# A gated mix of attention and a gMLP: whole-array products, shared key moments and a new order of loads

## The chip, the cores and the metric

The kernel runs on one core of one Trainium2 chip. The metric is the device time of one execution in microseconds (us). The core has five engines that run side by side, each through its own list of instructions in a fixed order: TensorE (PE in the profile; its weight loads are shown apart as PEld), VectorE (DVE), ScalarE (ACT), GpSimd (POOL) and SyncE (SP), which issues the DMAs. They wait for each other by semaphores.

## What is computed

`x` is 2048 x 512. A gate `g` weighs two branches. Branch a is attention with 32 heads of 16 dimensions that share one key and one value head. Branch b is a gMLP: a gelu, a layer norm over half of the columns, a product over the sequence with `w_sp`, and a gated projection.

```python
x = A_x
g = _sigmoid((x * gate_w).sum(-1, keepdims=True))
a = _A_ref(x, A_wq, A_wk, A_wv, A_wo)     # q @ k, softmax, @ v, then @ wo; 32 query heads, one k and v
b = _B_ref(x, B_w_in, B_w_sp, B_b_sp, B_w_out)
# inside _B_ref:
#   z = gelu(x @ w_in); z1 = z[:, :688]; z2 = layernorm(z[:, 688:])
#   out = (z1 * (w_sp @ z2 + b_sp)) @ w_out
return g * a + (1 - g) * b
```

The scores are small, so the kernel replaces the exponential by a polynomial of third degree. Numerator and denominator of the softmax then need only moments of the keys (sums over the 2048 positions of products of key components, with and without the value), computed once, and per query the products of its components.

## The kernel before

**Planner and queues.** The program is a list of tasks, each with an engine, an estimated cost, what it reads and writes, and a priority (a lower `pri` goes first). `Plan.run` (L241) plays them through a model of the engines and so fixes, when the program is built, the order of each engine's list. On the chip each engine keeps that order: an instruction that waits holds up what stands behind it. `after` makes a real wait, `opens` and `gates` only hold a task back in the model. SP's list of DMAs comes out of the same planning.

**Products.** `mm4` (L477 to 482) writes a product as four matmuls of 128 rows by 32 columns of the array, each with its own weight load, on the same moving data; they run side by side and are called a quad here. `mm1` (L485) uses the whole array of 128 by 128 in one matmul. `mmq` (L487 to 492) is a quad whose four parts have different weights or different moving data, and `half5` (L759 to 764) one whose parts take two halves of the moving data. In the profile L480 is `mm4`, L485 `mm1`, L490 `mmq`, L762 `half5`.

**Start.** Loads are issued in the order identity, first quarter of x, wk, wv, gate_w, second quarter, wq, the other quarters, win2 (the half of w_in for z2), constants, win1 (the half for z1) (L523 to 535). Per quarter, `g_x` transposes x, `g_kv` makes keys and values (and, with a 33rd column, the gate's sums), `moments` (L593 to 602) adds to the key moments, and `g_gate` makes the gate's sums in another layout. `moments` has per tile of 128 positions the large product for the third moments (bank K3), a correction, and three small quads that make the lower moments four times over for four groups of partitions (bank T). `moments_out` turns them into the weights T3, T3d, M2, T1b, T2b, TEb. `gate_out` runs the exponentials (L634 to 636), and the gelus of z2 (L746) come after them by `after=[ex_t[0]]`.

**Units.** There are 16 units u, each one group of eight heads by one quarter of the queries. `g_q` (L641) makes Q and writes it to DRAM (`qe`, four DMAs and a fifth for a rolled copy); `y_load` (L659) reads it back twice for each half e of a unit, spread over partitions, as Y and YB. POOL multiplies them to X (L691), two products with T3 follow (W, L696), and DVE multiplies their results by Y to Pr (L698). N and D, in banks of their own, then collect Q times T1b and T2b, E times TEb, X times M2 and T3d, and Pr times `sel` (L701 to 711); M2, T3d and `sel` are `mmq` quads. After each four units `g_den` (L717) makes the denominators and writes OT (L735).

**gMLP.** `g_z2` (L739) makes z2 with gelu, statistics, a power on POOL for the inverse deviation (L752, priority 0) and the normalisation on ACT (L756). `g_z1` makes z1. `g_sp` (L787) multiplies by the transposed `w_sp`, which comes in quarters by transposing DMAs (`ld_wT`, L776) into the space of x and of the key features. `g_out` (L817) makes four output tiles of each quarter.

**Order at the end of the builder (L835 to 883).** The four quarters of the start, moments and gate; then Q of units 0 to 3, all of z2, all of z1; then the units, with Q four units ahead, `w_sp` after units 0 and 1, the late weights (`ld_late`) after unit 2, and per four units `g_den`, `g_sp`, `g_out`.

Of the kernel before, what the change touches and what calls it, by code (L numbers as in the profile page):

```python
# [34 lines left out]
WARM = 5  # L35
# [7 lines left out]
SLACKS = {("pool", "pe"): 1200.0, ("dve", "pe"): 350.0, ("act", "pe"): 300.0}  # L43
# [3 lines left out]
DMA_ISSUE = 300.0  # L47


def constants():  # L50
# [29 lines left out]
    rol = np.eye(128) + bmq * ((p[:, None] + 8) % 16 == p[None, :] % 16)  # L80
# [4 lines left out]
    small = np.concatenate([sel.reshape(128, 128), hsel.reshape(128, 128), bmq, rol], 1)  # L85
# [103 lines left out]
class Task:  # L189
    __slots__ = ("alt", "fn", "deps", "users", "left", "pri", "grp", "first", "dma", "bytes", "chan", "tag", "idx",  # L190
                 "ready", "eng", "start", "end", "op", "rate", "opens", "gates")


class Plan:
# [8 lines left out]
    def add(self, eng, cost, fn, r=(), w=(), pri=50.0, grp=None, evac=False, dma=0, size=0, chan=None, rate=DMA_RATE, tag="", after=(), opens=()):  # L203
# [5 lines left out]
        t.users, t.op, t.eng = [], None, None  # L209
        r, w = list(r), list(w)  # L210
# [16 lines left out]
        t.gates = []  # L227
        for d in t.deps:
            d.users.append(t)
        for d in t.opens:  # L230
            d.users.append(t)
        t.left = len(t.deps) + len(t.opens)
# [8 lines left out]
    def run(self, prog, allowed):  # L241
# [5 lines left out]
        pipe = [0.0]  # L247
        busy = {e: 0.0 for e in ENG}
# [42 lines left out]
        while done < len(self.tasks):  # L291
# [51 lines left out]
            if t.dma:  # L343
                free[e] = now + cost
                st = max(pipe[0], now + DMA_ISSUE)
                pipe[0] = st + t.bytes / t.rate
# [24 lines left out]
def build_kernel(nc, x_d, wq_d, wk_d, wv_d, wo_d, win_d, wsp_d, bsp_d, wout_d, gw_d, out_d):  # L371
    es = ExitStack()
    with es:
# [32 lines left out]
        cs = sb("cs", [128, 512], B16)  # L406
# [10 lines left out]
        T1d = sb("T1d", [128, 1], F32)  # L417
        S0 = sb("S0", [128, 1], F32)
# [45 lines left out]
        rol = cs[:, 384:512]  # L464
        x2 = x_d.rearrange("b s d -> (b s) d")
        out2 = out_d.rearrange("b s d -> (b s) d")

        def diag(t):

            a = t[:, :, :]  # L470
            return bass.AP(tensor=a.tensor, offset=a.offset, ap=[a.ap[0], [48, 2], [1, 16]])
# [4 lines left out]

        def mm4(b, n, off, lhsT, rhs, start, stop):  # L477

            def f(t):
                return [t.matmul(ps[32 * q:32 * q + 32, 512 * b() + off:512 * b() + off + n], lhsT[:, 32 * q:32 * q + 32], rhs,  # L480
                                 start=start, stop=stop, tile_position=(0, 32 * q)) for q in range(4)]
            return f
# [4 lines left out]
        def mmq(b, n, off, lhsTs, rhss, start, stop):  # L487

            def f(t):
                return [t.matmul(ps[32 * q:32 * q + 32, 512 * b() + off:512 * b() + off + n], lhsTs[q], rhss[q],  # L490
                                 start=start, stop=stop, tile_position=(0, 32 * q)) for q in range(4)]
            return f
# [8 lines left out]
        nd = [0]  # L501

        def load(eng, fn, w, r=(), size=0, n=1, pri=0.0, chan=None, rate=DMA_RATE, tag="", after=()):
# [3 lines left out]
            return add(eng, 4500.0 if rate < DMA_RATE else 540.0 * n, fn, r=r, w=w, dma=16 * n, size=size, pri=pri, chan=chan, rate=rate, tag=tag, after=after)  # L507
# [8 lines left out]
        add("dve", 350.0, lambda v: v.memset(Pr[:, 0, 0, :], 0.0), w=[("Pr", 0)], pri=-1)  # L516
        gw_ = Group("any")
# [5 lines left out]
        load("sp", lambda q: q.dma_start(ident[:], id_d), ["id"], size=32768, pri=-1)  # L523
# [3 lines left out]
        load("sp", nonc(lambda q: q.dma_start(wkvg[:, :, 32:33], gw_d.rearrange("(dt p one) -> p dt one", p=128, one=1))), ["gw"], size=16384, pri=0)  # L527
        ld_x(1)
        load("sp", lambda q: q.dma_start(wq[:], wq_d.rearrange("(dt p) n -> p dt n", p=128)), ["wq"], size=524288, pri=1)
        ld_x(2)  # L530
        ld_x(3)
        load("sp", lambda q: q.dma_start(win[:, :, FH:F], win_d[:, FH:F].rearrange("(dt p) n -> p dt n", p=128)), ["win2"], size=704512, pri=4)
        load("sp", lambda q: q.dma_start(cf[:], cf_d), ["cf"], size=8704, pri=5)
        load("sp", lambda q: q.dma_start(cs[:], cs_d), ["cs"], size=131072, pri=5)
        load("sp", lambda q: q.dma_start(win[:, :, 0:FH], win_d[:, 0:FH].rearrange("(dt p) n -> p dt n", p=128)), ["win1"], size=704512, pri=6)
        add("pool", 300.0, lambda g: g.memset(bspz[:], 0.0), w=[("bspz", 0), ("bspz", 1)], pri=0)
        add("pool", 100.0, lambda g: g.memset(nhalf[:], -0.5), w=["nhalf"], pri=0)
        add("pool", 100.0, lambda g: g.memset(RK[:, :, 304:305], 1.0), w=["rk1"], pri=0)
        add("pool", 1600.0, lambda g: g.memset(kkD, 0.0), w=[("X", c) for c in range(4)], pri=0)
# [8 lines left out]
        add("dve", 100.0, lambda v: v.tensor_copy(gwr[:], wkvg[:, :, 32:33].broadcast_to([128, 4, 32])), r=["gw"], w=["gwr"], pri=0)  # L548
# [12 lines left out]
        def g_kv(c):  # L561
            g = Group("any")
            for k in range(4):
                for dt in range(4):
                    add("pe", 26.0, mm1(lambda g=g: g.b, 33, 64 * k, xT[:, dt, 512 * c + 128 * k:512 * c + 128 * k + 128], wkvg[:, dt, 0:33], dt == 0, dt == 3),
                        r=["wk", "wv", "gw", ("x", c, dt)], grp=g, pri=0, tag="kv")
# [5 lines left out]
            add("dve", 200.0, lambda v: v.tensor_copy(RK[:, t4, 272:304].rearrange("p k (e d) -> p k e d", e=2),  # L572
                                                      src()[:, :, 16:32].unsqueeze(2).broadcast_to([128, 4, 2, 16])),
                w=[("rv", c)], grp=g, evac=True, pri=0, tag="rv")
            add("dve", 130.0, lambda v: v.tensor_scalar(RK[:, t4, 256:272], src()[:, :, 0:16], 0.25, None, ALU.mult), w=[("rk", c)], grp=g, evac=True, pri=0, tag="rk")
            add("dve", 100.0, lambda v: v.tensor_scalar(gs[:, t4].unsqueeze(2), src()[:, :, 32:33], E_MAX, None, ALU.min), w=[("gs", c)], grp=g, evac=True, pri=0, tag="gs")
            kxa = kx[:, t4, 0:16]
            kxo = bass.AP(tensor=kxa.tensor, offset=kxa.offset, ap=[kxa.ap[0], [32, 4], [1, 16], [1, 8]])
            add("dve", 620.0, lambda v: v.tensor_tensor(psi[:, t4, :].rearrange("p k (r i) -> p k r i", i=8), kxa.unsqueeze(3).broadcast_to([128, 4, 16, 8]), kxo, ALU.mult),
                r=[("kx", c)], w=[("psi", c)], pri=1, tag="psi")  # L580
            add("dve", 1150.0, lambda v: v.tensor_tensor(RK[:, t4, 0:256].rearrange("p k (c d) -> p k c d", d=16), kxa.unsqueeze(3).broadcast_to([128, 4, 16, 16]),
                                                         RK[:, t4, 272:288].unsqueeze(2).broadcast_to([128, 4, 16, 16]), ALU.mult),
                r=[("kx", c), ("rv", c)], w=[("rkv", c)], pri=1, tag="rkv")
            add("pool", 450.0, lambda v: v.tensor_tensor(kkE[:, t4, :].rearrange("p k (e d) -> p k e d", e=2), kx[:, t4, 0:16].unsqueeze(2).broadcast_to([128, 4, 2, 16]),
                                                         kx[:, t4, 8:24].unsqueeze(2).broadcast_to([128, 4, 2, 16]), ALU.mult),
                r=[("kx", c)], w=[("kkE", c)], pri=1, tag="kkE")
            add("pool", 300.0, lambda v: v.tensor_scalar(kkD[:, t4, :].rearrange("p k (r i) -> p k r i", i=8)[:, :, :, 0], kkE[:, t4, 0:16], -1.0, None, ALU.mult),
                r=[("kkE", c)], w=[("X", c)], pri=1, tag="kkE")
# [4 lines left out]
        def moments(c):  # L593
            for k in range(4):
                kt = 4 * c + k
                st, sp_ = kt == 0, kt == 15
                rep = lambda a: [a] * 4
# [538 lines left out]
```

## Time and profile before

| | |
|---|---|
| median of 3 runs | 336.86 us (334.85 to 341.41) |
| the profiled execution | 337.39 us, of which the span from first to last instruction is 335.6 us |
| PE busy | 303.2 us, 6279 matmuls |
| DVE, POOL, ACT busy | 239.7, 165.9, 93.8 us |
| moved by DMA | 54.17 MB, 161 GB/s on average |

The profile is that of one execution. The span leaves out 1.8 us around the instructions. A busy PE is not PE at its peak: a matmul's row lasts until its last result is out, and the next one starts before that. So the pace of a stream of matmuls is read from the starts of neighbouring rows.

### The profile page before, as it was taken

The page shows a single profiled execution, that of the slowest core. Times are in us where ns is not written, and L with a number is a line of the kernel's source. Part 1 is how long each engine was busy: PE and PEld are TensorE (multiplying, and loading weights), DVE is VectorE, ACT ScalarE, POOL GpSimd, SP SyncE. Part 2 cuts the span into 40 slices and gives each one's busy share as a digit, 9 for nine tenths or more (in the row PEclk, how much of TensorE's full clock was granted, in tenths as well). Part 3 has the DMA queues.
Part 4 walks back from the last instruction along what each step waited for, and adds up shares of the span by engine and source line. Part 5 has one row for each costly group of instructions (what it writes and reads, how often), then busy time and mean ns, then how long its engine had stood idle before and what let it go on. Part 6 is the DMA issues. An engine that isn't in the chain of part 4 may idle for free.

```text
span 335.6 us, 13852 instructions
## 1 busy us (share of the span) xinstructions
PE 303.2 (90%) x6279; PEld 162.9 (49%) x6279; DVE 239.7 (71%) x335; ACT 93.8 (28%) x163; POOL 165.9 (49%) x156
## 2 busy tenths in 40 slices
PE   5976879899999997999999769988999999799993
PEld 2763345454445554564445335542565554244551
DVE  1855479998465798876949859849588977949522
ACT  2525467966655010113212002230100012000001
POOL 7421049656757284367484614376672487640000
PEclk9977899999999999999999999999999999999998
DMA  6956264999996899398999752988987579700002
GB/s 160 348 160 170 72 130 120 190 199 283 189 215 156 199 165 237 94 189 158 263 187 233 185 120 42 238 187 209 248 153 177 109 177 240 172 5 2 4 4 66
DMA packets 54472, 54.17 MB, mean 161 GB/s; under 512 B 36900, under 2 KB 45960, under 8 KB 54280
## 3 DMA queue, kind: packets, MB, share of 16 engines
q1 hardware_dynamic: 54408, 53.24, 68.6%
q8 instruction: 50, 0.82, 1.1%
q14 instruction: 14, 0.11, 0.1%
HBM read 40.65 MB, written 5.24 MB: 137 GB/s over the span
## 4 chain that ended last, share of the span: by engine, by line
PE 74%; DVE 12%; issue 6%; ACT 4%; DMA 1%; SPq 1%; DVEq 0%
PE ps L480 61%; PE ps L490 8%; DVE Pr L698 6%; PE ps L485 3%; ACT z L756 2%; PE ps L762 2%; DMA wkvg<-in_gate_w_dram 1%; ACT z L745 1%; DVE bst L747 1%; DVE z L801 1%; DVE win L735 0%; DVE nmr L753 0%; DVE Prd L713 0%; DVE Rh L728 0%; DVE outsb L828 0%
## 5 line engine op out<-in xcount | busy, mean ns | idle before, releaser
L691 POOL TENSOR_TENSOR X<-Y,YB 128x512 bf16<-128x512 bf16 x128 | 148.3, 1159 | 96.1 <-DMA Y<-qe 36.2
L698 DVE TENSOR_TENSOR Pr<-ps,Y 128x1024 bf16<-128x1024 f32 x128 | 152.3, 1215 | 32.3 <-issue 22.7
L480 PE MATMUL ps<-wT,z 128*32 128x512 bf16 x1280 | 85.0, 379 | 0.0
L480 PE MATMUL ps<-X,T 128*32 128x512 bf16 x1024 | 80.7, 380 | 4.1 <-DVE Pr L698 3.9
L480 PEld LDWEIGHTS ps<-wT,z 128*32 128x32 bf16 x1280 | 36.6, 97 | 30.0 <-issue 0.2
L480 PEld LDWEIGHTS ps<-X,T 128*32 128x32 bf16 x1024 | 26.9, 96 | 31.8 <-DVE Pr L698 12.6
L480 PE MATMUL ps<-win,xT 128*32 128x344 bf16 x512 | 25.0, 320 | 3.4 <-ACT z L745 2.9
L480 PE MATMUL ps<-wout,z 128*32 128x512 bf16 x384 | 26.2, 379 | 0.5 <-DVE z L804 0.5
L679 ACT ACTIVATE E<-ps 128x512 bf16<-128x512 f32 x16 | 9.5, 597 | 59.8 <-PE ps L480 56.1
L712 ACT ACTIVATE Ns<-ps 128x512 f32<-128x512 f32 x16 | 9.6, 599 | 58.1 <-PE ps L490 58.1
L648 ACT ACTIVATE Qt<-ps 128x512 bf16<-128x512 f32 x16 | 9.6, 597 | 47.2 <-PE ps L480 38.2
L827 ACT ACTIVATE outsb<-ps,G 128x512 bf16<-128x512 f32 x14 | 9.5, 687 | 41.5 <-PE ps L480 41.5
L480 PE MATMUL ps<-xT,win 128*32 128x512 bf16 x320 | 20.3, 380 | 0.5 <-ACT E L679 0.5
L801 DVE TENSOR_TENSOR z<-ps,z 128x512 bf16<-128x512 f32 x20 | 13.7, 683 | 9.7 <-PE ps L480 9.5
L490 PE MATMUL ps<-Pr,cs 128*32 128x512 bf16 x256 | 19.7, 379 | 0.5 <-DVE Pr L698 0.5
L735 DVE SCALAR_TENSOR_TENSOR win<-Ns,S,ps 128x512 bf16<-128x512 f32 x16 | 11.9, 745 | 10.9 <-PE ps L480 10.8
L480 PEld LDWEIGHTS ps<-win,xT 128*32 128x32 bf16 x512 | 12.6, 99 | 14.1 <-ACT z L745 7.0
L480 PE MATMUL ps<-xT,wq 128*32 128x512 bf16 x256 | 18.1, 400 | 0.6 <-ACT Q L656 0.2
L747 DVE BATCH_NORM_STATS2 bst<-z 128x6 f32<-128x344 bf16 x32 | 15.4, 505 | 4.0 <-ACT z L745 3.9
L480 PE MATMUL ps<-wo,win 128*32 128x512 bf16 x256 | 17.8, 379 | 0.0
L745 ACT ACTIVATE z<-ps 128x344 bf16<-128x344 f32 x32 | 14.0, 454 | 9.0 <-PE ps L480 7.9
L756 ACT ACTIVATE z<-z,nmr,rstd 128x688 bf16<-128x688 bf16 x16 | 15.0, 960 | 1.7 <-DVE nmr L753 1.6
(119 smaller groups left out, 314.6 us busy)
## 6 DMA issues: line engine op xcount, KB each, us to landing
Y<-qe SPq DMA_DIRECT2D x32, 512.0 KB, 5.2
YB<-qe SPq DMA_DIRECT2D x32, 512.0 KB, 6.7
wT<-in_A_x_dram SPq DMA_DIRECT2D x4, 512.0 KB, 6.1
qe<-Qt SPq DMA_DIRECT2D x64, 32.0 KB
out_dram<-outsb SPq DMA_DIRECT2D x16, 128.0 KB, 3.3
win<-in_B_w_in_dram SPq DMA_DIRECT2D x2, 688.0 KB, 8.8
qe<-qe SPq DMA_DIRECT2D x16, 64.0 KB
wout<-in_B_w_out_dram SPq DMA_DIRECT2D x1, 640.0 KB, 5.3
```

The costliest lines, as they stand in the source:

```text
L480: return [t.matmul(ps[32 * q:32 * q + 32, 512 * b() + off:512 * b() + off + n], lhsT[:, 32 * q:32 * q + 32], rhs, start=start, stop=stop, ...
L485: return lambda t: t.matmul(bank(b(), n, off), lhsT, rhs, start=start, stop=stop)
L490: return [t.matmul(ps[32 * q:32 * q + 32, 512 * b() + off:512 * b() + off + n], lhsTs[q], rhss[q], start=start, stop=stop, tile_position=( ...
L648: add({"act": (520.0, lambda a: a.activation(Qt[:, s, :], bank(g.b), ACT.Copy))}, 0, None, w=[("Q", s)], grp=g, evac=True, pri=1, tag="Qev")
L691: xf = lambda v, xi=xi, j=j, n=n: v.tensor_tensor(X[:, xi, :], Y[:, n % NY, j, :], YB[:, n % NYB, j, :], ALU.mult)
L698: add("dve", 1230.0, lambda v, gw=gw, pi=pi, n=n, j=j: v.tensor_tensor(Pr[:, pi, :, :], bank(gw.b, 1024).rearrange("p (t n) -> p t n", t=2 ...
L712: add({"act": (590.0, lambda a: a.activation(Ns[:, u % NNS, :], bank(gn.b), ACT.Copy))}, 0, None, w=[("Ns", u % NNS)], grp=gn, evac=True, ...
L735: add("dve", 750.0, lambda v, gr=gr, u=u, G=G: v.scalar_tensor_tensor(OT[:, tg % 2, G, :], Ns[:, u % NNS, :], S0[:, 0:1], bank(gr.b), ALU. ...
L745: add("act", 400.0, lambda a, g=g, h=h: a.activation(z2[:, FH * st + 344 * h:FH * st + 344 * h + 344], bank(g.b, 344), ACT.Gelu_apprx_tanh ...
L747: add("dve", 495.0, lambda v, h=h: v.bn_stats(bst[:, st, h, :], z2[:, FH * st + 344 * h:FH * st + 344 * h + 344]), r=[("z2", st, h)], w=[( ...
L756: add("act", 820.0, lambda a, s2=s2: a.activation(z2[:, FH * s2:FH * s2 + FH], z2[:, FH * s2:FH * s2 + FH], ACT.Identity, bias=nmr[:, s2:s ...
L801: add("dve", 690.0, lambda v: v.tensor_tensor(dst, bank(g.b), dst, ALU.mult), w=[("z1", ft, tc)], grp=g, evac=True, pri=3.5, tag="u")
```

## The change

1. **Whole-array products.** All `mm4` become `mm1`: Q, E, W, the products with T1b, T2b and TEb, z1, z2, `w_sp` (but for its last tile), out, and the spread of the denominators. `mmq` and `half5` stay quads. The planner adds `SWITCH` (100 ns) where PE goes from one kind to the other, and a penalty of 2.0 on the priority of a task that would switch.
2. **N and D of a quad in one run.** The products with M2 and T3d get `after=tp[3:]`, that is, they wait for the fourth Pr of their half, as those with `sel` do.
3. **Key cross-moments once, then spread.** Two whole-array products per tile in place of three quads and the correction; then `mT`, a copy in two bf16 parts, and six products with `spr` that spread them over the partitions. The key features `psi` and `rkv` may go to POOL as well as to DVE.
4. **Gate late.** gate_w is loaded after unit 0's Y loads. The gate's sums (16 quads, and 64 products of one column in `g_gs`) follow z1 in the list, and the exponentials wait for all gelus. A gelu on `ones` at the start loads its table.
5. **New order of loads.** wq follows wk; win1 comes after unit 0's loads; DMAs of units have priorities from 2.1 up, ahead of win2 (4) and of the rest. `hold` keeps others back in the model until the last Y load; no wait comes of it on the chip. The power on POOL has priority 11 in place of 0, and a `slack` of 4 us.
6. **Order of the units.** Q runs three units ahead, z1 stands after unit 0, `w_sp` quarters after units 1 and 3. Nine warming matmuls in place of five.

```diff
-WARM = 5
+WARM = 9
+SWITCH = 100.0
+YPRI = 2.1
+SWITCH_PRI = 2.0
...
-                k = (t.pri, t.idx)
+                k = (t.pri + (SWITCH_PRI if e == "pe" and t.tiles != tiles else 0.0), t.idx)
...
+            if e == "pe":
+                if t.tiles != tiles:
+                    cost += SWITCH
+                tiles = t.tiles
...
-        def mm4(b, n, off, lhsT, rhs, start, stop):
-
-            def f(t):
-                return [t.matmul(ps[32 * q:32 * q + 32, 512 * b() + off:512 * b() + off + n], lhsT[:, 32 * q:32 * q + 32], rhs,
-                                 start=start, stop=stop, tile_position=(0, 32 * q)) for q in range(4)]
-            return f
...
+        add("act", 1300.0, lambda a: a.activation(nmr[:, 0:1], ones[:, 0:1], ACT.Gelu_apprx_tanh), r=["ones"], w=["junk2"], pri=-2, tag="table")
...
+        load("sp", lambda q: q.dma_start(wq[:], wq_d.rearrange("(dt p) n -> p dt n", p=128)), ["wq"], size=524288, pri=0)
...
-                add("pe", c_mm(288), mm1(lambda: gK3.b, 288, 0, psi[:, kt, :], RK[:, kt, 0:288], st, False), r=[("psi", c), ("rkv", c), ("rk", c), ("rv", c)], grp=gK3, pri=1, tag="K3")
-                add("pe", 26.0, mm1(lambda: gK3.b, 16, 272, kkD[:, kt, :], RK[:, kt, 272:288], False, sp_), r=[("X", c), ("rv", c)], grp=gK3, pri=1, tag="K3")
-                add("pe", 30.0, mmq(lambda: gT.b, 49, 0, rep(kx[:, kt, :]), rep(RK[:, kt, 256:305]), st, False), r=[("kx", c), ("rk", c), ("rv", c), "rk1"], grp=gT, pri=1, tag="T")
-                add("pe", 26.0, mmq(lambda: gT.b, 16, 64, rep(kkE[:, kt, :]), rep(RK[:, kt, 272:288]), False, False), r=[("kkE", c), ("rv", c)], grp=gT, pri=1, tag="T")
-                add("pe", 26.0, mmq(lambda: gT.b, 1, 96, rep(RK[:, kt, 272:304]), rep(RK[:, kt, 304:305]), False, sp_), r=[("rv", c), "rk1"], grp=gT, pri=1, tag="T")
+                add("pe", c_mm(288), mm1(lambda: gK3.b, 288, 0, psi[:, kt, :], RK[:, kt, 16:304], st, sp_), r=[("psi", c), ("rkv", c), ("rk", c), ("rv", c)], grp=gK3, pri=1, tag="K3")
+                add("pe", 30.0, mm1(lambda: gT.b, 49, 0, RK[:, kt, 193:321], RK[:, kt, 272:321], st, False), r=[("rkv", c), ("rk", c), ("rv", c), "rk1"], grp=gT, pri=1, tag="T")
+                add("pe", 26.0, mm1(lambda: gT.b, 16, 49, kkD[:, kt, :], RK[:, kt, 288:304], False, sp_), r=[("X", c), ("rv", c)], grp=gT, pri=1, tag="T")
...
+            for i, (off, lo, n) in enumerate(((0, 0, 49), (64, 49, 16), (96, 48, 1))):
+                for z in range(2):
+                    add("pe", 30.0, lambda t, i=i, off=off, lo=lo, n=n, z=z: t.matmul(bank(gT2.b, n, off), spr[:, i, :], mT[:, z, lo:lo + n], start=i == 0 and z == 0, stop=i == 2 and z == 1),
+                        r=["cs", "mTh", "mTl"], grp=gT2, pri=1, tag="T2")
...
-            ex_t[0] = add("act", 2200.0, ex, r=[("gs", c) for c in range(4)], w=["Er", "E"], pri=-1, tag="gate")
+            ex_t[0] = add("act", 2200.0, ex, r=["gs"], w=["Er", "E"], pri=5, tag="gate", after=[t for t in pl.tasks if t.tag in ("gelu1", "gelu2")])
...
-                        add("pe", c_mm(512), mm4(lambda gw=gw, t=t: gw.b + t, 512, 0, T3[:, t, :], X[:, xi, :], True, True),
+                        add("pe", c_mm(512), mm1(lambda gw=gw, t=t: gw.b + t, 512, 0, T3[:, t, :], X[:, xi, :], True, True),
...
-                add("pe", c_mm(512), mmq(lambda: gn.b, 512, 0, [M2[:, e, :]] * 4, [X[:, i, :] for i in xs], False, False), r=["M2"] + xr, grp=gn, pri=pr_, tag="N")
+                add("pe", c_mm(512), mmq(lambda: gn.b, 512, 0, [M2[:, e, :]] * 4, [X[:, i, :] for i in xs], False, False), r=["M2"] + xr, grp=gn, pri=pr_, tag="N", after=tp[3:])
...
-w=[("rstd", st // 4)], pri=0, tag="pow")
+w=[("rstd", st // 4)], pri=11, tag="pow", slack=4000.0)
...
-        for u in range(4):
+        for u in range(2):
             q_and_guard(u)
         for st in range(NST):
             g_z2(st)
-        for ft in range(6):
-            for tc in range(4):
-                g_z1(ft, tc)
...
-                if u < 2:
-                    ld_wT(u)
+                if u == 0:
+                    ld_win1()
+                    for ft in range(6):
+                        for tc in range(4):
+                            g_z1(ft, tc)
...
+                    for c in range(4):
+                        g_gate(c)
+                    for st in range(NST):
+                        g_gs(st)
+                    gate_out()
+                    q_and_guard(2)
+                if u in (1, 3):
+                    ld_wT(u // 2)
                 if u == 2:
                     ld_late()
-                if u + 4 < 16:
-                    q_and_guard(u + 4)
+                if u + 3 < 16:
+                    q_and_guard(u + 3)
```

More of the change, by code (lines that the diff above doesn't have):

```diff
@@ L190 @@
     __slots__ = ("alt", "fn", "deps", "users", "left", "pri", "grp", "first", "dma", "bytes", "chan", "tag", "idx",
-                 "ready", "eng", "start", "end", "op", "rate", "opens", "gates")
+                 "ready", "eng", "start", "end", "op", "rate", "opens", "gates", "tiles", "slack")
 class Plan:
@@ L201, in __init__, with add @@
         self.readers = {}
-    def add(self, eng, cost, fn, r=(), w=(), pri=50.0, grp=None, evac=False, dma=0, size=0, chan=None, rate=DMA_RATE, tag="", after=(), opens=()):
+    def add(self, eng, cost, fn, r=(), w=(), pri=50.0, grp=None, evac=False, dma=0, size=0, chan=None, rate=DMA_RATE, tag="", after=(), opens=(), hold=(), slack=0.0):
         t = Task()
@@ L209, in add @@
         t.users, t.op, t.eng = [], None, None
+        t.tiles = getattr(fn, "tiles", 1)
         r, w = list(r), list(w)
@@ L226, in add @@
         t.opens = [self.lastw[k] for k in opens]
-        t.gates = []
+        t.gates = list(hold)
+        t.slack = slack
         for d in t.deps:
             d.users.append(t)
-        for d in t.opens:
+        for d in t.opens + t.gates:
             d.users.append(t)
-        t.left = len(t.deps) + len(t.opens)
+        t.left = len(t.deps) + len(t.opens) + len(t.gates)
         for k in r:
@@ L247, in run @@
         pipe = [0.0]
+        tiles = 1
         busy = {e: 0.0 for e in ENG}
@@ L345, in run @@
                 st = max(pipe[0], now + DMA_ISSUE)
-                pipe[0] = st + t.bytes / t.rate
+                pipe[0] = st + t.bytes / (DMA_FIRST if st < 16000.0 and t.rate == DMA_RATE else t.rate)
                 t.end = pipe[0] + DMA_LAT
@@ L491, in f @@
                                  start=start, stop=stop, tile_position=(0, 32 * q)) for q in range(4)]
+            f.tiles = 4
             return f
@@ L501, in build_kernel, with load @@
         nd = [0]
-        def load(eng, fn, w, r=(), size=0, n=1, pri=0.0, chan=None, rate=DMA_RATE, tag="", after=()):
+        yld = [None]
+        def load(eng, fn, w, r=(), size=0, n=1, pri=0.0, chan=None, rate=DMA_RATE, tag="", after=(), hold=()):
             if chan is None:
@@ L506, in load @@
                 nd[0] += 1
-            return add(eng, 4500.0 if rate < DMA_RATE else 540.0 * n, fn, r=r, w=w, dma=16 * n, size=size, pri=pri, chan=chan, rate=rate, tag=tag, after=after)
+            return add(eng, 4500.0 if rate < DMA_RATE else 540.0 * n, fn, r=r, w=w, dma=16 * n, size=size, pri=pri, chan=chan, rate=rate, tag=tag, after=after, hold=hold)
         def nonc(fn):
@@ L581, in g_kv @@
[L581 to L586, printed above, removed]
@@ L776, in ld_wT @@
         def ld_wT(tc):
-            load("sp", lambda q: q.dma_start(bspz[0:1, tc % 2, :], bsp_d[512 * tc:512 * tc + 512].rearrange("(one t) -> one t", one=1)), [("bspz", tc % 2)], size=4096, pri=13, chan="bsp%d" % (tc % 2), after=[yld[0]] if tc < 2 else [])
+            load("sp", lambda q: q.dma_start(bspz[0:1, tc % 2, :], bsp_d[512 * tc:512 * tc + 512].rearrange("(one t) -> one t", one=1)), [("bspz", tc % 2)], size=4096, pri=13, chan="bsp%d" % (tc % 2), hold=[yld[0]] if tc < 2 else [])
             for k in range(4):
@@ L790, in g_sp @@
             n = 512 if ft < 5 else 256
-            mk = mm4 if ft < 5 else half5
-            add("pe", c_mm(n), mk(lambda: g.b, 512, 0, ones, bspz[:, tc % 2, :], True, False), r=["ones", ("bspz", tc % 2)], grp=g, pri=pri, tag="sp", opens=[("z2", i, 1) for i in range(NST)] + [("wT", tc % 2, k) for k in range(4)])
+            mk = mm1 if ft < 5 else half5
+            add("pe", c_mm(n), mk(lambda: g.b, 512, 0, ones[:], bspz[:, tc % 2, :], True, False), r=["ones", ("bspz", tc % 2)], grp=g, pri=pri, tag="sp", opens=[("z2", i, 1) for i in range(NST)] + [("wT", tc % 2, k) for k in range(4)])
             for st in range(NST):
```

159 lines of the change are left out of this document (87 added, 72 removed).

## The prediction

> **What bounds the kernel now.** I read the page first (shares, slices, chain), then two long stretches, then what PE waits for, then single rows for paces.
>
> ```profile
> span 335.6 us, 13852 instructions
> ...
> PE 303.2 (90%) x6279; PEld 162.9 (49%) x6279; DVE 239.7 (71%) x335; ACT 93.8 (28%) x163; POOL 165.9 (49%) x156
> ...
> PE 74%; DVE 12%; issue 6%; ACT 4%; DMA 1%; SPq 1%; DVEq 0%
> ```
>
> PE carries three quarters of the chain and is busy for 90%; no other engine passes 71%. So the end moves by what PE is spared or what it loses. But busy is not peak, so I need the pace. The timeline of PE gives it, in a dense stretch:
>
> ```profile
> 309.59 1.68 PE L480 MATMUL ps<-wT,z 128*32 128x512 bf16 x28
> 311.10 0.39 PE L490 MATMUL ps<-Pr,cs 128*32 128x512 bf16 x4
> ...
> 50.79 0.90 PE L480 MATMUL ps<-win,xT 128*32 128x344 bf16 x20
> 51.52 0.39 PE L480 MATMUL ps<-X,T 128*32 128x512 bf16 x4
> ...
> 318.70 0.62 PE L480 MATMUL ps<-Rh,sg 128*32 128x128 bf16 x32
> 319.14 0.39 PE L480 MATMUL ps<-wo,win 128*32 128x512 bf16 x4
> ```
>
> 28 matmuls, 7 quads, lie between two starts 1.51 us apart: 0.216 us for a quad of 512 columns (0.42 ns per column). 5 quads of 344 columns take 0.73 us, 0.146 each; 8 of 128 columns 0.44 us, 0.055 each. All three are the same rate per column. A quad already runs as fast as its moving data pass. One whole-array matmul passes the same columns, so **part 1 saves no streaming time**; it saves instructions only.
>
> With these paces I compare work and time at the start:
>
> ```profile
> 0.00:50.00 50.00, 37.43 (x781) 23.18 (x781) 27.32 (x75) 22.43 (x42) 16.87 (x28) 0.90 0.62 173
> 50.00:330.00 280.00, 265.20 (x5494) 139.67 (x5498) 210.93 (x258) 70.12 (x122) 148.99 (x129) 1.00 0.72 161
> ...
> L480 PE MATMUL ps<-win,xT 128*32 128x344 bf16 x224 | 11.1, 333 | 0.9 <-ACT z L745 0.5 <-DVE qm L851 0.4
> L480 PE MATMUL ps<-xT,wq 128*32 128x512 bf16 x96 | 7.6, 433 | 0.2 <-ACT Q L656 0.2
> L485 PE MATMUL ps<-ident,wT 128*128 128x128 bf16 x64 | 6.2, 274 | 2.2 <-DMA wT<-in_A_x_dram 2.2
> ```
>
> (Stretches: length, busy us of PE, PEld, DVE, ACT, POOL, then clock, DMA share, GB/s; then PE's groups in the first 50 us.) At full rate the groups are 56 x 0.146 = 8.2, 24 x 0.216 = 5.2 and 64 x 0.055 = 3.5 us; the smaller ones are about 7.4 more by the same paces (an estimate). That is 24.3 us of work in 50: **25.7 us are lost at the start**, about half of what PE loses in the whole span. The reasons stand in the timelines:
>
> ```profile
> 7.46 0.45 DVE L548 COPY gwr<-wkvg 128x128 bf16<-128x128 bf16 x1 [3.78 <-DMA wkvg<-in_gate_w_dram]
> ...
> 25.24 0.61 ACT L635 ACTIVATE Er<-Er 128x512 f32<-128x512 f32 x1
> ...
> 27.05 1.28 ACT L745 ACT_TABLE_LOAD   x1
> 31.28 0.46 ACT L745 ACTIVATE z<-ps 128x344 bf16<-128x344 f32 x1 [2.95 <-PE ps L480]
> ...
> 34.25 0.43 DVE L607 TENSOR_TENSOR T<-ps,cf 128x256 bf16<-128x256 f32 x1 [1.71 <-PE ps L485]
> ...
> 46.23 1.04 POOL L752 TENSOR_TENSOR rstd<-ve,nhalf 128x4 f32<-128x4 f32 x1 [19.51 <-DVE ve L751]
> 47.50 1.15 POOL L691 TENSOR_TENSOR X<-Y,YB 128x512 bf16<-128x512 bf16 x1 [0.23 <-POOL rstd L752]
> ```
>
> DVE waits for gate_w before it frees x; the first gelu comes at 31.28, behind the exponentials; POOL stands 19.5 us at the power, with X queued behind it, so units begin at 47.5 although T3 was made at 34.25. After 50 us what PE waits for is this (us in total, times, longest):
>
> ```profile
> PE ps L490 <- issue: 5.0, 2, 3.1
> PE ps L480 <- issue: 4.1, 3, 2.7
> PE ps L480 <- DVE Pr L698: 3.9, 9, 0.8
> PE ps L480 <- ACT z L745: 3.1, 5, 1.5
> ...
> PE ps L480 <- DVE Prd L713: 1.2, 2, 1.0
> ```
>
> **The change part by part**, against the profiled execution's 337.4 us (335.6 and 1.8 around it; 0.5 above the median shown).
>
> *Start (parts 4, 5, 6): minus 14.* Win2's load is issued at the head of the list as before:
>
> ```profile
> win<-in_B_w_in_dram SPq DMA_DIRECT2D x2, 688.0 KB, 8.8
> ```
>
> Its issue at about 6.7 and 8.8 us to landing let z2 start near 15.5. Before that PE can do the transposes, keys, two Q and some moments, some 7.5 us of work, so 8 are lost. From there z2 holds 512 / 4 x 0.146 = 18.7 us of work that waits neither for the exponentials nor the table, and covers DVE's key features. Products of moments that stand in PE's list before their features are ready hold up z2 behind them; I allow 4 us. So 12 of 25.7 are still lost. Ends: minus 5, only the wait for gate_w (3.8) and the table load (1.3); minus 18, nothing lost after 15.5. I take 14, nearer to the upper end, because POOL's wait (19.5) and the late gelu both go. SP now issues Q's four writes, the copy and four Y loads of unit 0 ahead of win2 if Q is ready by then; wq ahead of x's second quarter delays that by its 512 KB. Gate_w, its 16 quads and the exponentials come under z1 and the units; if ACT is late there, G1 is what out waits for, long after.
>
> *Instructions (part 1): minus 2.3.* PE stands at "issue", with no semaphore open, in the middle of groups:
>
> ```profile
> 131.92 0.40 PE L480 MATMUL ps<-bspz,ones 128*32 128x512 bf16 x4 [1.12 <-issue]
> ...
> 197.75 0.24 PE L480 MATMUL ps<-Rh,sg 128*32 128x128 bf16 x4 [2.65 <-issue]
> ...
> q8 instruction: 50, 0.82, 1.1%
> ```
>
> The queue of instructions moves 0.82 MB for the page's 13852 instructions, of which PE has twice 6279, so I read these as waits for code. By the diff 4880 matmuls at L480 become 1220, and the total about 2500, 40%. Of the 3.8 us after the start, 60% go. Ends: 0 and minus 3.8.
>
> *Late waits (parts 5, 6): minus 6.8.* A wait costs its idle time plus the tail of the quad before it: a quad's row lasts 0.39 (at 51.52), its successor could start after 0.216, so 0.17. Nine waits for Pr and two for Prd: 3.9 + 1.2 + 11 x 0.17 = 7.0; those for z2's gelus after the start 3.1 - 0.5 + 4 x 0.17 = 3.3. Units that begin some 20 us sooner give DVE that lead; z2 will be done before the units crowd in. I take 3.3 whole and half of 7.0, as DVE and PE stay nearly matched. Ends: 0 and minus 10.3.
>
> *Switches (part 1): plus 11.1.* Almost all work was of one kind; now each run of quads has a switch on both sides. Rows from the start show its price:
>
> ```profile
> 22.89 0.24 PE L490 MATMUL ps<-xT,gwr 128*32 128x128 bf16 x4
> 23.06 0.18 PE L485 MATMUL ps<-wT,X 128*128 128x16 bf16 x1
> ...
> 23.81 0.17 PE L485 MATMUL ps<-wT,X 128*128 128x16 bf16 x1
> 23.84 0.28 PE L485 MATMUL ps<-wT 128*128 128x288 bf16 x1
> 23.96 0.17 PE L485 MATMUL ps<-wT,X 128*128 128x16 bf16 x1
> 24.06 0.21 PE L490 MATMUL ps<-wT 128*32 128x49 bf16 x4
> ```
>
> After 16 columns the next matmul of the same kind starts 0.03 us on, one of the other kind 0.10: plus 0.07. After a quad of 128 columns the next of its kind came after 0.055, the whole-array one after 0.17: plus 0.115. Together 0.185 per run. (The row at 23.84 also shows that a whole-array matmul of 288 columns, with its own weights, takes 0.12 us, 0.42 ns per column: the rate of the quads, with the larger weight load hidden.) Part 2 makes 32 runs of four quads; q2 adds up to 16, the denominators 4, the last tiles of z1 and `w_sp` 8 or a few more: 60 runs, 11.1. Ends: 32 runs, 5.9; 260 quads each alone, 48. I take 60, since the penalty of 2.0 keeps equal quads together.
>
> The Trainium skill (TensorEngine Tiling, Tiling Modes) says that a change of tiling mode drains TensorE. Taken as the whole tail, that price would be 0.17 on each side and the sum 9.3 higher; the rows above show 0.07 and 0.115, so the measured price stands, and the drain is a rival below.
>
> *The rest: plus 0.4.* `g_gs` adds 64 matmuls of about 0.025 (from the 0.03 above), 1.6; part 3 removes 48 small quads at that pace, 1.2. The spread (two DVE copies, six matmuls, under 1 us) delays T1b and T2b only; T3 does not wait for it. Part 2's new wait puts M2 and T3d behind the fourth Pr: D ends later, Prd follows, and the next unit's T2b waits for that bank; four Pr of the next half cover it. X's buffers come free later, and POOL (49%) has the room.
>
> Sum: 337.4 - 14 - 2.3 - 6.8 + 11.1 + 0.4 = 325.8; less 0.5 to compare with the median, **325.3 us**.
>
> **The rivals.**
> - *More is given back* (311). All ends together: 18, 3.8, 10.3 and 32 runs: 337.4 - 32.1 + 5.9 + 0.4 - 0.5 = 311. For it: PE would be dense from 15 us on. Against: a static order made from estimates never fitted so well here.
> - *The whole tail at each switch* (335). 60 x 2 x 0.17 = 20.4 in place of 11.1. For it: matmuls of 512 columns were hardly switched before, so their drain is not shown. Against: the small ones above.
> - *The gain stays at the start* (341). POOL also waited 36.2 us for Y:
>
> ```profile
> POOL X L691 <- DMA Y<-qe: 36.2, 13, 10.1
> ```
>
> If early Y loads collide with x and win2, units begin no sooner, the start gives its lower end of 5 and late waits remain: 337.4 - 5 - 2.3 + 11.1 + 0.4 - 0.5 = 341. Against: DMA's share in the first 50 us is 0.62.
> - *Slower: the runs fall apart* (362). Where `sel`, M2, T3d, q2 and the last tiles switch one by one, 260 x 0.185 = 48 in place of 11.1. It equals the time before at 122 runs and is 2% slower from 158. For it: before, M2 and T3d stood apart among other work; a W pair that gets ready between two quads costs one more run. Against: the common wait of part 2.
>
> **How the numbers follow.** Forecast (318 to 331) 0.52; more given back 0.14; whole tail 0.10; stays at the start 0.12; slower 0.12. A measurement of this kernel tells about 2% from no change: 330.1 and 343.6 us. Faster: nine tenths of the first and all of the second, 0.61. Within 2%: the rest of the first, the tail and the start, 0.27. Slower: 0.12. The range, 311 to 341, leaves out the slower case and a little more; the forecast's own is 318 to 331.
>
> **What would show it.** Right: the first X before 30 us, the first gelu of z2 before 20, no wait of POOL for `ve`; a whole-array matmul every 0.216 us; "issue" waits of PE below 4 us; some 60 runs of quads with 0.16 to 0.19 lost at each; PE dense from 16 us on. Wrong: a pace above 0.22 us for a whole-array matmul, over 100 runs, or units that still begin after 40 us.

## The result and the profile after

The changed kernel takes **324.35 us** (median of 4 runs, 323.98 to 324.71). The kernel before, run beside it, takes 335.91 us (4 runs, 334.85 to 341.41). The ratio is 0.967, 95% interval 0.962 to 0.971: faster by 3.3%, and 0.95 us below the forecast of 325.3. Here and below the ratios leave out, on both sides, executions over 1.5% longer than the fastest of their kernel, so they can differ a little from the quotient of the medians. The profiled execution took 324.12 us, its span is 322.3.

The page of the changed kernel first (busy us and instructions of each engine; the queue that brings code):

```profile
span 322.3 us, 6349 instructions
...
PE 307.1 (95%) x2517; PEld 138.9 (43%) x2517; DVE 237.3 (74%) x333; ACT 92.5 (29%) x163; POOL 167.4 (52%) x156
...
q8 instruction: 21, 0.34, 0.5%
```

2517 matmuls in place of 6279, and PE is busy for 95% in place of 90%. The same two stretches as before, cut at PE's last products (length, busy us of PE, PEld, DVE, ACT, POOL, then clock, DMA share, GB/s):

```profile
0.00:50.00 50.00, 45.04 (x400) 24.58 (x401) 40.54 (x104) 32.07 (x63) 28.93 (x36) 1.00 0.81 209
50.00:317.00 267.00, 261.96 (x2118) 114.35 (x2116) 195.66 (x229) 59.72 (x100) 138.46 (x121) 1.00 0.69 160
```

In the first 50 us the DMA share is 0.81 in place of 0.62, and the clock granted to TensorE is 1.00 in place of 0.90. The 0.90 of the kernel before comes from two stretches at half the clock, each at one of its two long issue waits of the start (1.83 us until 18.60, 3.13 us until 30.70):

```profile
19.28:22.69 3.41, 3.41 (x85) 2.84 (x82) 2.02 (x6) 1.48 (x3) 1.33 (x2) 0.50 0.55 171
29.52:36.35 6.83, 5.65 (x72) 2.63 (x76) 2.74 (x12) 1.89 (x4) 0.00 (x0) 0.50 0.65 169
```

PE is busy for 9.1 us in them with work that takes 4.7 at full rate: some 4 us more are lost there (an estimate). The changed kernel has no such stretch before PE's last product.

That the units start earlier stands in the timeline of POOL:

```profile
21.81 0.48 POOL L591 TENSOR_TENSOR X<-wT 128x64 bf16<-128x64 bf16 x1
30.16 4.85 POOL L709 TENSOR_TENSOR X<-Y,YB 128x512 bf16<-128x512 bf16 x4 [7.87 <-DMA YB<-qe]
35.18 4.84 POOL L709 TENSOR_TENSOR X<-Y,YB 128x512 bf16<-128x512 bf16 x4 [0.17 <-POOL X L709]
40.10 2.10 POOL L771 TENSOR_TENSOR rstd<-ve,nhalf 128x4 f32<-128x4 f32 x2
```

The first X comes at 30.16 in place of 47.50. What POOL waits for now is the load of YB; the power stands behind eight X and waits for nothing. On ACT the gelus of z2 start at 15.36, where they started at 31.28:

```profile
15.36 0.46 ACT L764 ACTIVATE z<-ps 128x344 bf16<-128x344 f32 x1 [0.74 <-PE ps L494]
```

What PE itself still waits for (us in total, times, longest):

```profile
PE ps L494 <- ACT E L697: 2.3, 3, 1.4
PE ps L494 <- ACT z L764: 1.4, 2, 1.0
PE ps L494 <- DVE Pr L716: 1.3, 4, 0.5
```

The two rows of "issue", 9.1 us in 5 waits before, are gone. The waits for Pr fell from 3.9 to 1.3, those for z2's gelus from 3.1 to 1.4. What came in their place is in PE's timeline, here one run of four quads (L499) between whole-array products (L494):

```profile
46.61 0.60 PE L494 MATMUL ps<-X,T 128*128 128x512 bf16 x2
47.13 0.40 PE L499 MATMUL ps<-X,M 128*32 128x512 bf16 x4
47.36 0.39 PE L499 MATMUL ps<-X,T3d 128*32 128x512 bf16 x4
47.58 0.60 PE L499 MATMUL ps<-Pr,cs 128*32 128x512 bf16 x8
48.11 0.39 PE L494 MATMUL ps<-E,TEb 128*128 128x512 bf16 x1
48.34 0.38 PE L494 MATMUL ps<-Qt,cs 128*128 128x512 bf16 x1
```

A neighbour of the same kind starts after 0.22 to 0.23 us. The two W products at 46.61 take 0.52 until the first quad starts, the two quads at 47.58 take 0.53 until the whole-array product starts: 0.216 for one and 0.30 to 0.31 for the one ahead of the switch. Over the whole trace the median is 0.309 before a quad and 0.312 after one, so a switch costs 0.093 or 0.096 at 512 columns. There are 126 of them (63 runs of quads): 11.8 us.

**Where the time came from.** I add up for each trace what the recorded matmuls need at full rate (0.216 us for 512 columns, 0.146 for 344, 0.108 for 256, 0.056 for 128, 0.025 at least; a quad as one product), and call the rest lost. Warming matmuls count as lost at the start.

| step | forecast | measured | how measured |
|---|---|---|---|
| start | -14 | -12.8 | lost in the first 50 us: 25.8 before, 13.0 after |
| instructions and late waits | -9.1 (-2.3 and -6.8) | -12.3 | lost after 50 us: 22.3 before; 20.7 after, of which 114 switches are 10.7 |
| switches | +11.1 | +10.7 | 114 of the 126, at 0.094; the others lie in the start, as did all of the kernel before |
| the rest | +0.4 | +1.0 | more work: 64 products of one column and 6 for the spread, less 32 small ones of the moments |
| behind PE's last product | 0 | +0.2 | 5.2 before, 5.4 after |
| sum | -11.6 | -13.2 | spans: 335.6 to 322.3 |

The medians differ by 11.6 only: the profiled execution of the kernel before took 1.5 us more than the median beside the change. The start's 12.8 are 2.7 before 16 us (9.9 lost before the change, 7.2 after) and 10.1 from there to 50 us (15.9 and 5.8).

### The profile page after: what moved, and what is told of

The parts are those of the page before. It is cut to its first block, busy times and chain, and to the rows that moved or that the text cites. A ratio compares the mean times of both kernels' runs of the same rounds, so it can differ in the third digit from the quotient of the medians.

```text
span 322.3 us, 6349 instructions
## 1 busy us (share of the span) xinstructions
PE 307.1 (95%) x2517; PEld 138.9 (43%) x2517; DVE 237.3 (74%) x333; ACT 92.5 (29%) x163; POOL 167.4 (52%) x156
## 4 chain that ended last, share of the span: by engine, by line
PE 48%; DVE 3%; issue 0%; ACT 0%; DVEq 0%
PE ps L494 40%; PE ps L499 6%; DVE Pr L716 2%; PE ps L781 2%; DVE outsb L847 0%; DVE Rf L745 0%; ACT E L697 0%; DVE z L823 0%; DVE qm L868 0%; PE ps L920 0%; DVEq L1087 0%; DVEq L172 0%
## 5 line engine op out<-in xcount | busy, mean ns | idle before, releaser
L494 PE MATMUL ps<-wT,z 128*128 128x512 bf16 x320 | 81.9, 380 | 0.0
L494 PE MATMUL ps<-X,T 128*128 128x512 bf16 x256 | 76.4, 381 | 1.4 <-DVE Pr L716 1.3
L494 PEld LDWEIGHTS ps<-wT,z 128*128 128x128 bf16 x320 | 30.6, 98 | 35.4 <-issue 0.6
L494 PEld LDWEIGHTS ps<-X,T 128*128 128x128 bf16 x256 | 21.9, 98 | 32.4 <-DVE Pr L716 6.9
L494 PE MATMUL ps<-wout,z 128*128 128x512 bf16 x96 | 26.7, 380 | 0.5 <-DVE z L823 0.5
L494 PE MATMUL ps<-win,xT 128*128 128x344 bf16 x128 | 22.6, 310 | 1.6 <-ACT z L764 1.4
L494 PE MATMUL ps<-xT,win 128*128 128x512 bf16 x80 | 20.5, 380 | 1.4 <-ACT E L697 1.4
L732 DVE SCALAR_TENSOR_TENSOR Prd<-ps,T1d,Qt 128x512 bf16<-128x512 f32 x16 | 11.9, 747 | 11.3 <-PE ps L499 11.3
L499 PE MATMUL ps<-Pr,cs 128*32 128x512 bf16 x256 | 19.5, 379 | 0.0
L494 PE MATMUL ps<-wo,win 128*128 128x512 bf16 x64 | 18.6, 380 | 0.2
L494 PE MATMUL ps<-xT,wq 128*128 128x512 bf16 x64 | 17.0, 379 | 0.6 <-DMA wkvg<-in_A_wv_dram 0.6
L494 PEld LDWEIGHTS ps<-win,xT 128*128 128x128 bf16 x128 | 10.9, 97 | 11.6 <-ACT z L764 5.2
```

Of the source, the lines that this page charges most:

```text
L494: return lambda t: t.matmul(bank(b(), n, off), lhsT, rhs, start=start, stop=stop)
L732: add("dve", 750.0, lambda v: v.scalar_tensor_tensor(Prd[:, u % NPD, :], bank(gd.b), T1d[:, 0:1], Qt[:, s, :], ALU.add, ALU.mult), r=["T1d ...
```

## The experiments

Times are medians. The kernel before took 334.32 us beside E1 to E4, 335.68 beside E5 to E8 and 336.16 beside E9 to E12.

### What the whole-array products are worth

**E1: the changed kernel with quads in its steady products, in the same order.**

```diff
+        def mm4(b, n, off, lhsT, rhs, start, stop):
...
+                return [t.matmul(ps[32 * q:32 * q + 32, 512 * b() + off:512 * b() + off + n], lhsT[:, 32 * q:32 * q + 32], rhs,
+                                 start=start, stop=stop, tile_position=(0, 32 * q)) for q in range(4)]
...
-                        add("pe", c_mm(512), mm1(lambda gw=gw, t=t: gw.b + t, 512, 0, T3[:, t, :], X[:, xi, :], True, True),
+                        add("pe", c_mm(512), mm4(lambda gw=gw, t=t: gw.b + t, 512, 0, T3[:, t, :], X[:, xi, :], True, True),
```

(and so for Q, E, T1b, T2b, TEb, z1, z2, `w_sp`, out and the denominators)

> The changed kernel with every one of its whole-array 512, 344 and 128 column products written as four 32-column matmuls again, and each engine's order left as it is. By the program 34 changes of kind are left of 126, and PE's instructions rise from 2517 matmuls to about 6150. Theory A (a change of kind costs 0.094 us, code fetch costs some us): 324.35 - 92 x 0.094 = 315.7 from the switches, plus 4 to 9 us of waits for code as before: 320 to 325, with waits at issue of 1 to 3 us inside groups again. Theory B (the whole-array products themselves are the gain): 330 or more. Theory C (code fetch is nothing, switches are all): 316.

Measured: 323.38 us (320.44 to 324.12), ratio 0.965 (0.955 to 0.975). That is the time of the changed kernel, and inside theory A's range. Only 33 switches are left, so about 9 us are saved. They are paid back, in part by PE's own waits in this profile:

```profile
PE ps L496 <- DVE Pr L723: 2.3, 7, 0.7
PE ps L496 <- issue: 2.1, 4, 0.9
PE ps L788 <- issue: 1.4, 1, 1.4
```

3.5 us of issue waits are back, and the waits for Pr are 1.0 us longer. In the first 50 us 15.2 us are lost in place of 13.0; there PE waits 1.3 us for wq's load, and from 8.43 to 11.85 the granted clock is 0.50. Behind PE's last product it takes 1.5 us more. So **part 1 by itself moves the time by about nothing in this order**; the gain comes with parts 2 to 6.

**E2: the kernel before with whole-array products, in its own order.**

```diff
-                        add("pe", c_mm(512), mm4(lambda gw=gw, t=t: gw.b + t, 512, 0, T3[:, t, :], X[:, xi, :], True, True),
+                        add("pe", c_mm(512), mm1(lambda gw=gw, t=t: gw.b + t, 512, 0, T3[:, t, :], X[:, xi, :], True, True),
```

(and so for all `mm4`)

> The kernel before with every product of its four-part helper as one whole-array matmul, all else and every engine's order as before. 228 changes of kind in place of 22. Theory A: 206 x 0.094 = 19.4 us more, less 5 to 9 us of waits for code: 345 to 351 us, slower. Theory B (whole-array products are the gain): under 330. The price of a change of kind in its rows: 0.09 to 0.10 us on each side.

Measured: 341.33 us (340.23 to 342.89), ratio 1.021 (1.012 to 1.031): slower, but less than expected. 228 switches in place of 22 cost 19 us, and 12 of these came back. Two timelines show from where some of them came. PE before, then POOL of E2:

```profile
27.23 0.33 PE L490 MATMUL ps<-wT 128*32 128x16 bf16 x24
30.70 0.22 PE L490 MATMUL ps<-wT 128*32 128x16 bf16 x8 [3.13 <-issue]
```

```profile
38.82 1.04 POOL L745 TENSOR_TENSOR rstd<-ve,nhalf 128x4 f32<-128x4 f32 x1 [14.39 <-DVE ve L744]
40.09 4.85 POOL L684 TENSOR_TENSOR X<-Y,YB 128x512 bf16<-128x512 bf16 x4 [0.23 <-PE ps L478]
```

Before, PE stood for 3.13 us in the middle of a group of moments, with no semaphore open. In E2 no issue wait is longer than 0.3, the clock of its first 50 us is 1.00, and the first X comes at 40.09 in place of 47.50 with loads and priorities unchanged. About 20 us are lost in its first 50 in place of 25.8. So a part of what the start lost before was the same kind of wait that the prediction counted only after 50 us, with the half clock behind it.

**E9 and E10: whole-array products of 512 columns cut into two and into four, in the same order.** They tell the number of instructions from the switches.

```diff
-            return lambda t: t.matmul(bank(b(), n, off), lhsT, rhs, start=start, stop=stop)
+            w = n // 2 if n == 512 else n
+            return lambda t: [t.matmul(bank(b(), w, off + i), lhsT, rhs[:, i:i + w], start=start and i == 0, stop=stop and i + w == n) for i in range(0, n, w)]
```

(E10: `n // 4`)

> The changed kernel with each whole-array product of 512 columns issued as two of 256 with the same weights, order, waits and switches unchanged; some 1000 matmuls more, 3500 in all. The pace of 256 columns was 0.108 to 0.110 us in the changed kernel, so the stream itself grows by 0 to 4 us. Theory A (the time that the quads cost beside the switches comes with the number of instructions that TensorE has to fetch): issue waits over 0.5 us come back, 1 to 2 us in all, and the time is 326 to 330. Rival (it comes with the quads' four small weight loads or their order, not with the count): no such waits, 324 to 328 by the pace alone.

> The same with four matmuls of 128 columns per product: about 5700 matmuls, near the 6177 of the quads. The pace of 128 columns was 0.056, so four take 0.224 in place of 0.216: about plus 9 us over some 1050 products. Theory A: issue waits of 3 us or more in all, runs that scatter by over 3 us, the instruction queue's bytes back at about 0.8 MB, and a time of 336 to 342. Rival: runs within 1 us of each other, issue waits as in the changed kernel, 331 to 334.

Measured: E9 325.76 us (325.51 to 326.09), ratio 0.975 (0.966 to 0.984); E10 333.51 us (331.14 to 338.63, 10 runs), ratio 0.997 (0.992 to 1.003). E9's pace is 0.109 per half, so its 964 products of two halves took about 2 us more, and the time grew by 1.4; its only issue wait of PE is 0.2 us: the rival. E10's pace is 0.056 per quarter, 7.7 us more, which gives 332; two of its runs lie below that. Its page has

```profile
PE 314.7 (95%) x5409; PEld 268.2 (81%) x5409; DVE 237.7 (72%) x333; ACT 92.6 (28%) x163; POOL 167.7 (51%) x156
...
q8 instruction: 44, 0.72, 0.9%
```

but its only issue wait of PE is 0.4 us. So the number of instructions alone did not bring the long waits back in this execution (theory A falls on that point). A scatter came as theory A had it: 7.5 us, and 4.4 without the slowest run, against 0.7 in the changed kernel; why is not shown.

### What the common wait is worth

**E3: M2 and T3d wait for their X alone.**

```diff
-... tag="N", after=tp[3:])
+... tag="N")
...
-... tag="D", after=tp[3:])
+... tag="D")
```

> The changed kernel without the two waits of the M2 and T3d products for the fourth Pr. 170 changes of kind in place of 126. Theory A: 44 x 0.094 = 4.1 us more, 328.5. Rival: D's bank and the X buffers come free sooner, which takes that back: 322 to 325.

Measured: 329.48 us (328.42 to 330.01), ratio 0.986 (0.978 to 0.995). 170 switches in place of 126: 44 x 0.094 = 4.1, and the time rose by 5.1 (theory A). A wait that was added saves 5 us here; some 4 of them because it keeps the quads together.

**E8: the same in quads** (planned for quads as in E5, both edits joined).

> The replanned kernel of four-part products without the waits of M2 and T3d for the fourth Pr. Theory A (the wait is there only to keep runs of equal kind together, and costs nothing by itself): within 1 us of the replanned kernel with the wait. Rival (D's bank and the X buffers profit): 1.5 to 4 us less.

Measured: 329.75 us (327.29 to 333.95, 10 runs), ratio 0.991 (0.984 to 0.998), 2 us below E5 and inside the scatter of both. It does not tell the two theories apart; in quads no gain of the wait shows.

### What the order at the start is worth

**E4: the kernel before, with the power late.**

```diff
-... w=[("rstd", st // 4)], pri=0, tag="pow")
+... w=[("rstd", st // 4)], pri=11, tag="pow", slack=4000.0)
```

(and `slack` in the planner as in the change)

> The kernel before with one edit: the power on POOL has priority 11 and 4 us of slack, as in the changed kernel. Theory A (POOL's wait of 19.5 us held the units back and that was a large part of the loss at the start): first X at about 36 us in place of 47.5, time 329 to 333. Rival: z2 and its gelus, behind the exponentials and the table, set the pace until 50 us whatever POOL does: 335 to 337.

Measured: 329.3 us (326.97 to 333.94), ratio 0.983 (0.974 to 0.993). This one edit, in the old order, is worth about half of the whole gain (theory A). In its profile the power is out of X's way, and X starts 12 us sooner than before:

```profile
24.78 1.46 POOL L588 TENSOR_SCALAR X<-wT 128x64 bf16<-128x64 bf16 x1
35.22 4.85 POOL L692 TENSOR_TENSOR X<-Y,YB 128x512 bf16<-128x512 bf16 x4 [8.98 <-PE ps L481]
```

**E6: the changed kernel with the power first again.**

```diff
-... w=[("rstd", st // 4)], pri=11, tag="pow", slack=4000.0)
+... w=[("rstd", st // 4)], pri=0, tag="pow")
```

> The changed kernel with the power on POOL at priority 0 and no slack again. By the program two X products, not eight, then stand ahead of the first power. Theory A (the early load order already made units early, the power matters less now): 325 to 329, POOL waiting 3 to 6 us for the variance. Rival (the power was all of it): 332 or more.

Measured: 324.21 us (324.13 to 324.67), ratio 0.980 (0.974 to 0.986). No effect: both expectations missed. POOL's timeline shows why:

```profile
30.44 2.38 POOL L709 TENSOR_TENSOR X<-Y,YB 128x512 bf16<-128x512 bf16 x2 [8.12 <-PE ps L494]
32.90 1.01 POOL L771 TENSOR_TENSOR rstd<-ve,nhalf 128x4 f32<-128x4 f32 x1
```

The first X is there ahead of the power in spite of the priority. A task of high priority can only go first if it is ready, and in the new order Y comes before the statistics of z2. So theory A's direction held, but not its 3 to 6 us of waiting. The edit that was worth 5 us in the old order is worth nothing in the new one.

**E7: the changed kernel with the gate early**, as in the kernel before: gate_w among the first loads, its quads with each quarter, the exponentials ahead of the gelus.

```diff
+            g_gate(c)
+            for st in range(4 * c, 4 * c + 4):
+                g_gs(st)
         moments_out()
+        gate_out()
...
+        load("sp", nonc(lambda q: q.dma_start(wkvg[:, :, 32:33], gw_d.rearrange("(dt p one) -> p dt one", p=128, one=1))), ["gw"], size=16384, pri=0)
...
...
-... grp=g, evac=True, pri=1, tag="gelu2")
+... grp=g, evac=True, pri=1, tag="gelu2", after=[ex_t[0]])
```

> The changed kernel with the gate as before: gate_w loaded after wv, the gate's sums in the four quarters, the exponentials ahead of the gelus of z2. Theory A (the gate late is worth the wait for the exponentials and a table load, 2 to 5 us at the start): 326 to 329. Rival (z2 is bound by win2's landing and ACT anyway): 323 to 325.5.

Measured: 325.32 us (325.12 to 325.74), ratio 0.984 (0.977 to 0.990). Part 4 is worth 1 us beside the rest, the rival's value.

### Other orders

**E5: the quads of E1, with the planner told that they are quads** (`f.tiles = 4` in `mm4`), so that it makes an order of its own.

> The changed kernel with its large products as four 32-column matmuls, and the planner told so, so that it plans without the price of the switches that are gone (some 32 changes of kind are left). Theory A: what the first experiment gained in switches (8.6 us) it lost to waits for code and to an order made for other costs; a fitting order gets 2 to 4 us back: 319 to 322, with 3 to 5 us of waits at issue left. Theory B (the gain and the loss of part 1 are equal whatever the order): 323 to 325.

Measured: 331.7 us (327.52 to 337.58, 11 runs), ratio 0.995 (0.989 to 1.001). Both expectations missed, 8 us above E1. The profiled execution is the longest of the 11, so it explains little; it has 9.7 us of issue waits of PE, and in its first 50 us 3.8 us less of work are done than in E1, though X starts at 30.24. What of this holds for the median stays open. So the gain of E1 hangs on its order: with quads and an order of their own, parts 2 to 6 keep little of it.

**E11 and E12: the changed kernel with another penalty for a switch.**

```diff
-SWITCH_PRI = 2.0
+SWITCH_PRI = 1.0
```

(E12: 8.0)

> The changed kernel with the penalty for a switch 1.0 in place of 2.0: another order, 114 switches in place of 126 (1.1 us at 0.094 each). The planner puts its end 3.2 us sooner. Theory that the end of the whole-array kernels follows the plan: 321 to 322. Rival that only the switches count and the rest of the plan's gain is an artefact of its estimates: 323 to 324.

> The same with a penalty of 8.0: 120 switches, the plan 2.9 us sooner. Following the plan: 321 to 322. Rival: 323.5 to 324.5, or later where work of high priority waits behind runs of the other kind.

Measured: E11 322.97 us (322.0 to 323.06), ratio 0.967 (0.958 to 0.975); E12 322.31 us (321.93 to 323.07), ratio 0.965 (0.956 to 0.974). All eight runs lie below the four of the changed kernel (323.98 and up), by 1.4 and 2.0 us at the median, though these were not taken beside it. They lie between the two expectations, E11 nearer the rival's, E12 nearer the plan's. E12 has 120 switches; the six fewer are 0.6 us. PE's waits changed too:

```profile
PE ps L494 <- DVE Pr L716: 1.0, 3, 0.6
...
PE ps L494 <- ACT E L697: 0.5, 1, 0.5
```

The waits for E fell from 2.3 to 0.8 (a second row, at L499, has 0.3) and those for z2's gelus from 1.4 to 0.4; others grew, and all of PE's waits together fell from 9.2 to 8.0. That E12 beats the changed kernel is likely; the ratios alone do not separate them.

## Why the prediction was right

The time, the sign and the likeliest case came out. The steps held to different degrees, and errors of opposite sign helped the sum.

- **No streaming time saved by part 1.** Right: the pace of a whole-array product of 512 columns is 0.216 at the median, that of a quad was 0.216. The Trainium skill (TensorE: Matmul & The Clock Gate, "Wait — 56ns, not 53.3ns?") gives 215.7 and 55.6 ns for 512 and 128 columns at full clock; the 0.216 and 0.056 of this trace agree.
- **Start, minus 14.** The size was nearly right (12.8), the division among causes was not, and that the size came out all the same is partly luck. The prediction put the loss down to the order alone. Its table of waits "after 50 us" is that of the whole execution: the row of 5.0 us in 2 lies at the start, inside the 25.7 us, and the half clock behind these two waits (some 4 us) has no term, though the row of the stretch shows 0.90. E2 shows that fewer instructions in the old order bring X from 47.5 to 40.1 and take some 5 us off the loss. E4 shows the power's place in the old order (X at 35.2), E6 that it no longer decides in the new one. E7 leaves 1 us for the gate. The two waits stood in the small quads of the moments, which part 3 takes out (they stay away in E1, whose longest issue wait in the first 50 us is 0.7). And the first 16 transposes take 1.05 us in place of 1.87, behind nine warming matmuls in place of five, with a pause of 0.4 us in between in place of 2.2. No run tells part 3, the order of the loads, the order of the units and the warming from each other.
- **Instructions, minus 2.3.** Too small: the term scaled the waits with the number of instructions, 60%, but all went, the end of the range (3.8). E10 speaks against the scale: at 5409 matmuls the count would have kept most of them, and 0.4 us were left in its profile.
- **Late waits, minus 6.8.** They gave what is left of 12.3, that is 8.5, inside the range (0 to 10.3). The half taken for Pr was too little: these waits fell by two thirds. That the early start of the units gave DVE the lead fits this, but no run shows it alone.
- **Switches, plus 11.1.** Right in price and number: 63 runs at 0.19 in place of 60 at 0.185. The two sides were taken as 0.07 and 0.115 and are 0.093 and 0.096, so that the sum fits so closely is partly luck. The small matmuls of the start did tell the size of the price for 512 columns, and the rival with the whole tail (0.17 on each side) fell; of the drain that the Trainium skill (TensorEngine Tiling (Array Packing), Tiling Modes) names, 0.093 to 0.096 shows. E3 confirms the price from the other side, and shows that the slower rival (runs that fall apart) would have been real: 44 more switches cost 5.1 us.
- **The rest, plus 0.4.** It came to 1.0: part 3 also adds a product per tile, so that 32 small ones go and not 48.
- **The signs in the trace.** X before 30 missed narrowly (30.16). The gelus before 20, no wait for `ve`, a pace of 0.216, no issue wait of 4 us, some 60 runs: as told. PE is not quite dense from 16 us on: 5.8 of the 34 us to 50 are lost.

What the prediction did not see is that in this order switches and whole-array products cancel. It had minus 2.3 and plus 11.1 for part 1, a loss of 8.8, and would have called E1 faster than the change by as much; measured, the two are level. What is paid back in E1 is issue waits (3.5 us), the start (2.2), the end (1.5) and waits for Pr (1.0).

## What to carry to other kernels

Price each edit within the order it will run in: the same edit of the power was worth 5 us in the old order (E4) and nothing in the new one (E6), and a wait that keeps like work together was worth 5 us (E3). After changing the kind of the steady work, run the planner's constants through again: another penalty gave perhaps 2 us more (E12).

## What the hardware showed

**A change between quads and whole-array products costs 0.07 to 0.11 us**, by size: 0.093 from a whole-array product of 512 columns to a quad, 0.096 back, 0.106 behind a quad of 128 columns, and 0.07 from a whole-array product of one column. It is less than the tail of the matmul ahead (0.17).

**Issue waits come in more than one kind of place.** The stretches of the two longest waits of the kernel before and of one in E1 (columns as above):

```profile
27.40:30.60 3.20, 0.17 (x24) 0.05 (x9) 0.63 (x1) 0.94 (x1) 0.00 (x0) 0.83 0.19 51
...
195.00:197.70 2.70, 0.10 (x8) 0.00 (x0) 0.47 (x1) 0.00 (x0) 0.00 (x0) 1.00 0.74 182
```

```profile
239.50:241.00 1.50, 0.18 (x5) 0.00 (x0) 0.24 (x1) 0.52 (x1) 1.42 (x2) 1.00 1.03 295
```

Some come while the DMA engines have little to do (0.19), in groups of quads of 16 columns, which use up instructions fastest (a quad in 0.03 us). Others come at a DMA share of 0.74 and more, in E5 in groups of 512 columns too (1.36 at 62.85, share 0.93), though one of 344 columns comes at 0.36 (1.75 at 49.43). E10 has such shares (1.26 from 238 to 244), and its quarters of 128 columns use up two instructions (one load, one matmul) in 0.056 us, as many per us as a quad's eight in 0.216; yet it hardly waits. So neither the count, the rate nor the DMA load explains all of them, and the cause stays open; shown is that they went with the whole-array products (9.1 us in the kernel before, waits of 0.3 at most in E2; 3.5 in E1, none in the changed kernel).

**A pause can halve the clock.** The two stretches of the kernel before stand above: a clock of 0.50 for 3.41 us behind a pause of 1.83, and for 6.83 us from within one of 3.13. In E5's profiled execution PE stood for 2.09 us at "issue", and the row of the stretch behind it shows a granted clock of 0.53:

```profile
123.40 1.04 PE L496 MATMUL ps<-Rh,sg 128*32 128x128 bf16 x32 [2.09 <-issue]
```

```profile
123.40:127.00 3.60, 3.60 (x71) 2.23 (x74) 1.49 (x2) 0.00 (x0) 0.98 (x1) 0.53 1.04 234
```

So the work in these 3.6 us took about twice its time, and such a pause cost 1.7 us beyond itself. In all traces, each of the ten stretches at half clock between the warm-up and PE's last product begins in a pause of PE of 1.1 to 3.1 us or less than 0.7 us behind one, whether PE stood at "issue" (E4, 1.76 and 2.28) or waited for another engine or a load (E5, 2.18 for X; E10, 1.49 for wq). The Trainium skill (TensorE: Matmul & The Clock Gate, What's actually happening) has the same half rate after an idle window of about 3.4 us; here 2.09 sufficed. It does not always follow: in the kernel before, the clock stayed at 1.00 behind the 2.65 us that ended at 197.75. What decides is not shown.
